# Where a kernel's end loads its MLP results and runs its last value products

## The chip, the cores and the metric

The kernel runs on one core of one Trainium2 chip. The time is the device time of that core in microseconds (us): the median of three runs, 750.84 us (750.7 to 752.2). The profile is one execution of the same program.

## The reference

One row block of 2048 tokens with 512 features goes through two branches that a gate mixes.

```python
def _A_ref(x, wqkv, wo):                      # H = 32 heads of 16, window W = 256
    q, k, v = ...                             # x @ wqkv, split into heads
    scores = jnp.einsum("bhqd,bhkd->bhqk", q, k) * (Dh ** -0.5)
    mask = (idx[:, None] - idx[None, :] >= 0) & (idx[:, None] - idx[None, :] < W)
    p = _softmax(jnp.where(mask[None, None], scores, -1e9), axis=-1)
    o = jnp.einsum("bhqk,bhkd->bhqd", p, v)
    return (...o...) @ wo

def _B_ref(x, w1, b1, w2, b2):                # F = 1792
    h = _gelu(jnp.einsum("bsd,df->bsf", x, w1) + b1)
    return jnp.einsum("bsf,fd->bsd", h, w2) + b2

g = _sigmoid((x * gate_w).sum(-1, keepdims=True))
return g * _A_ref(...) + (1 - g) * _B_ref(...)
```

## The kernel before

**Two streams of work share TensorE.** The dense stream is a generator, `dense()`: the projections to q, k and v for four row blocks `t` of 512 tokens, then the MLP in eight turns (four row blocks, two halves of the hidden features; products `u` into the hidden features, `y` out of them), then `final(t)`, which multiplies the normalised attention output `ot` of a row block with `wo` (products `a`), mixes in the gated MLP result and stores. Each dense product is three matmuls (`mm3`, lines 108 to 110), because operands are kept as a high and a low part.

**The attention stream** runs over units `u`: eight groups `g` of four heads, and in each 16 blocks `kb` of 128 keys. For each unit there are four matmuls `sm` (line 519) whose row maxima VectorE takes, and, 12 units later (`LEAD`), four matmuls `st` (line 564) whose exponentials ScalarE writes to `pt` (line 586) and VectorE clips to the window (line 574, in the last 12 units). Every fourth unit a block of about 47 value products `pv` (line 608) multiplies the `pt` of six key blocks with the values in `vbuf`. The result `nd` is stored to DRAM; `att_norm` later loads the denominators (`den`), takes their reciprocal on VectorE (line 650), stores that (`RD`), loads numerators and reciprocals (`num`, `rb`), multiplies, and stores `OT`, from which `load_part` fetches `ot`.

**What sets the order.** Python writes all engines' instructions in one pass, and each engine runs its own in that order. A loop over `u` writes `st` and value products and lets the dense stream fill in `step / 4` ns of products after each; smaller work (exponentials, stores, `att_norm`) is put on a heap with `after(ns, ...)` and written when a running count of nominal ns passes its due time. So a change of position in the loop moves instructions on every engine. All loads and stores are issued by SyncE, on one DMA queue.

**PSUM.** The pools `st` and `sm` have three buffers each. The value products take one buffer from each of them, so with `st` before them they use the buffer of the `st` three places back. The dense products alternate between two buffers `d`.

**The end.** The maxima run 12 units ahead, so they are through before the last 12 units of the other loop. `load_y(t)` then fetches the MLP results of row blocks 0, 1 and 2 from DRAM (`YB`) into the buffers that the maxima used (`qd`, `kd`): six loads of 512 KB. In the version before, that is written at units 9, 11 and 13 of the last group, two loads at each. Value products of unit `u - 1` are written inside unit `u`, right behind its third `st`, and those of the last unit stand behind the loop, ahead of all of `final`.

```python
if op == "p" and i == PVAT and u >= 1:     # line 944
    att_pvs(u - 1)
if u - NU + NKB in (9, 11, 13):            # line 958
    load_y((u % NKB - 9) // 2)
att_pvs(NU - 1)                            # line 960, behind the loop
```

Of the kernel before, what the change touches and what calls it, by code (L numbers as in the profile page):

```python
# [32 lines left out]
def gated_mix(ctx: ExitStack, tc: tile.TileContext, x, wqkv, wo, w1, b1, w2, b2, gate_w, out):  # L33
# [12 lines left out]
    def f32(ap):  # L46
        return ap.bitcast(F32)
# [67 lines left out]
    def after(ns, fn, *args):  # L115
        now[1] += 1
        heapq.heappush(todo, (now[0] + ns, now[1], fn, args))

    def step_todo():
        due, _, fn, args = heapq.heappop(todo)  # L120
        keep, now[0] = now[0], due
        fn(*args)
        now[0] = max(keep, due)

    def tick(ns):
        now[0] += ns
        while todo and todo[0][0] <= now[0]:
            step_todo()

    def need(*keys):  # L130
        for key in keys:
            while key not in done:
                step_todo()
# [319 lines left out]
    def ready(t, g_, k):  # L453
        need(*[("qk", t, k * NC + 2 * (g_ // 4) + a) for a in range(2)])

    def part(st, g_, s):

        return heads(st, g_)[s].rearrange("d u a c -> (d u) (a c)")
# [23 lines left out]
    def load_kd(g_, c):  # L482
        for t in range(max(c - 1, 0), c + 1):
            ready(t, g_, 1)
            k0 = 0 if t == c else T - W
            at = W if t == c else 0
            src = heads(SK[t], g_)[:, :, :, :, k0:].rearrange("s d u a c -> (s d u) a c")
            nc.sync.dma_start(f32(kd[0:96, slot(g_, c), :, at:at + T - k0]), src)

    def load_qd(g_, c):  # L490
        ready(c, g_, 0)
        put_pairs([f32(qd[48 * s:48 * s + 48, slot(g_, c)]) for s in range(2)], SQ[c], g_)

    def load_qs(g_, c):
        ready(c, g_, 0)
        need(("v", NT - 2, NB - 1))
        for s in range(2):
            v = f32(qs[64 * s + 4:64 * s + 52, :, c * T:(c + 1) * T])
            nc.sync.dma_start(v, part(SQ[c], g_, s).rearrange("r (a c) -> r a c", a=2))
# [8 lines left out]
    def att_max(g_, b, i):  # L508

        if b % RB == 0 and (g_, b // RB) not in Ms:  # L510
            Ms[g_, b // RB] = sb.tile([128, 2 * RB, 2], F32, tag="M", bufs=2, name=f"M{g_}_{b}")
        M = Ms[g_, b // RB]
        hb, pr = divmod(i, 2)
        c, n = b // NB, slot(g_, b // NB)
        j = 2 * (b % NB) + hb
        w = min(64 * (2 * b + hb + 1), W + 64)
        k1 = 64 * (j + 1) + W
        p = ps.tile([128, 320], F32, tag="sm", bufs=3, name=f"sm{g_}_{b}_{i}")
        nc.tensor.matmul(p[:, :w], qd[0:96, n, pr, 128 * j:128 * (j + 1)], kd[0:96, n, pr, k1 - w:k1],  # L519
                         start=True, stop=True)  # L520
        junk = cs.tile([128, 320], BF16, tag="jm", bufs=1, name=f"jm{g_}_{b}_{i}")

        def red():
            nc.vector.tensor_tensor_reduce(junk[:, :w], p[:, :w], mask[:, 320 - w:320], 1.0, -3e38,  # L524
                                           ALU.add, ALU.max, M[:, 2 * (b % RB) + hb, pr:pr + 1])
            done.add(("max", g_, b, i))
        tick(w / 2.4 + 13)
        after(100, red)
# [63 lines left out]
    def att_pvs(u):  # L592

        g_, kb = divmod(u, NKB)
        c, k = divmod(kb, NB)
        if k < NB - 1:
            return
        blocks = list(range(max(kb - 5, 0), kb + 1))
        pairs = list(zip(blocks, reversed(blocks) if c else blocks))
        n = g_ * NT + c - 1  # L600
        if n >= 0:
            need(("nd", *divmod(n, NT)))
        pv = [ps.tile([128, T], F32, tag=tag, bufs=3, name=f"pv{g_}_{c}_{tag}") for tag in ("st", "sm")]

        def mm(b, i, hf, q, e, rhs, start, stop):
            r = 64 * (1 ^ hf ^ i % 2)
            v = 68 * (b % NB) + 17 * (i % 2 * 2 + i // 2)
            nc.tensor.matmul(pv[r // 64][32 * i:32 * i + 32, q - c * T:e - c * T],  # L608
                             vts[g_, b // NB][r:r + 64, v:v + 32], rhs(r),
                             start=start, stop=stop, skip_group_check=True, tile_position=(r, 32 * i))  # L610
        if c == 0:
            for i in range(4):
                mm(0, i, 1, 0, 64, lambda r: nil[r:r + 64].broadcast_to([64, 64]), True, False)
        for j, pair in enumerate(pairs):
            for hf, b in enumerate(pair):
                need(("pt", g_, b, hf))
            ends = []
            for i in range(4):
                for hf, b in enumerate(pair):
                    k0 = b * 128 + hf * 64  # L620
                    q, e = max(k0, c * T), min(k0 + W + 64, S, (c + 1) * T)
                    mm(b, i, hf, q, e, lambda r: pts[g_, b][r:r + 64, hf, i // 2, q - k0:e - k0],
                       j == 0 and not (c == 0 and hf == 1), j == len(pairs) - 1)
                    ends.append(e - q)
            tick(max(ends) * 1.6 + 40)
        nd = sb.tile([128, T], F32, tag="tmp", bufs=3, name=f"nd{g_}_{c}")

        def half():
            nc.scalar.activation(nd, pv[0], AF.Copy)

        def ev():
            nc.vector.tensor_add(nd, nd, pv[1])
            after(HOLD if g_ * NT + c < NQ - 4 else 800, store)

        def store():
            nc.sync.dma_start(ND[c][g_ // 2][g_ % 2], nd)
            done.add(("nd", g_, c))
            if g_ % 2 == 1:
                after(NORM if g_ * NT + c < NQ - 4 else 3500, att_norm, c, g_ // 2)
        after(100, half), after(700, ev)  # L640
# [200 lines left out]
    def load_y(t):  # L841

        need(*[("y", 1, t, b) for b in range(NB)])
        for i in range(NB // 2):
            if t < 2:
                v = f32(qd[:, t, i]).rearrange("p (j f) -> p j f", j=2)
            else:
                v = f32(kd[:, i, :, 0:T])
            nc.sync.dma_start(v, YB[t].rearrange("(i j p) f -> i p j f", j=2, p=128)[i])
            for j in range(2):  # L850
                ybs[t * NB + 2 * i + j] = v[:, j]
# [44 lines left out]
    def dense():  # L896
        for t in range(NT):
            yield from qkv(t)
        for n in range(len(TURNS)):
            yield from mlp(n)  # L900
        yield None
        for t in range(NT):
            yield from final(t)

    stage = ["qk"]
    run = dense()
# [13 lines left out]
    NU = NG * NKB  # L920
# [5 lines left out]
    for u in range(-LEAD, NU):  # L926
        m = u + LEAD
        gm, bm = divmod(m, NKB)
        step = STEP if u >= 0 else STEP0
        for i in range(4):  # L930
            if i == 1 and m % NB == 0 and NB <= m < NU - NB:
                load_kd(*divmod(m // NB + 1, NT)), load_qd(*divmod(m // NB + 1, NT))
            if i % 2 == 0:
                pair = (i, i + 1) if stage[0] != "u" else (i,)
            elif len(pair) == 2:
                continue
            else:
                pair = (i,)
            for op, i in [(op, k) for k in pair for op in ORDER[:3]] + [("f", k) for k in pair]:
                if op == "s" and u >= 0:  # L940
                    att_exp(u // NKB, u % NKB, i)
                if op == "m" and m < NU:
                    att_max(gm, bm, i ^ XOR)
                if op == "p" and i == PVAT and u >= 1:
                    att_pvs(u - 1)
                if op == "f":
                    fill(step / 4)
        if m < NU and bm % RB == RB - 1:
            after(900, att_rows, gm, bm // RB)
        if m % NB == QAT % NB and QAT <= m < QAT + NKB:  # L950
            load_qs(0, (m - QAT) // NB)
        if u % NB == 0 and NB <= u < NU - NB:
            load_ks(*divmod(u // NB + 1, NT))
        if u % NB == 2 and NB < u < NU - 3 * NB:
            load_qs(*divmod(u // NB + 3, NT))
        if u % NB == 0 and u >= 0:
            att_load_v(*divmod(u // NB, NT))
        if u - NU + NKB in (9, 11, 13):
            load_y((u % NKB - 9) // 2)
    att_pvs(NU - 1)  # L960
    for c in run:
        tick(c or 0)
    tick(1e9)


# [6 lines left out]
NKB = S // 128  # L972
# [3 lines left out]
LEAD = 12  # L976
# [19 lines left out]
AHEAD = 9e3  # L996
STEP0 = 2750.0
PVAT = 2
STEP = 2330.0
_TC = dict()  # L1000
_INS = ["A_x", "A_wqkv", "A_wo", "B_w1", "B_b1", "B_w2", "B_b2", "gate_w"]
# [18 lines left out]
```

## Time and profile before

| | |
|---|---|
| median of three runs | 750.84 us (750.7 to 752.2) |
| profiled execution: its time, its span | 750.61 us, 748.9 us |
| TensorE busy | 734.0 us, 98% of the span |
| VectorE, ScalarE, GpSimd busy | 520.6, 421.7, 372.4 us |
| granted TensorE clock | 1.00 over the whole span |
| chain that ended last | TensorE 84%, DMA 4%, VectorE 4%, ScalarE 3%, issue 3% |

The span is the profiled stretch of that execution; 1.7 us of its time lie outside. A matmul is listed with the time from its start to its modelled end, but the next one starts before that end: a product of 128x512 is listed at about 0.39 us and the following one starts 0.23 us later. Distances between starts are therefore what counts on TensorE. A time in brackets at a row is the engine's idle time ahead of it and what ended that.

### The profile page before, as it was taken

How to read it: one execution, taken by the hardware profiler on the slowest of the kernel's cores; microseconds unless marked ns; L12 is line 12 of the kernel's file. 1: busy time of each engine (PE TensorE's matmuls, PEld its weight loads, DVE VectorE, ACT ScalarE, POOL GpSimd, SP SyncE). 2: the span in 40 equal slices, each digit the busy share in tenths (PEclk: the TensorE clock that was granted, in tenths of full speed). 3: DMA queues.
4: the chain of work that ended last, by engine and by line, in shares of the span. 5: the costliest groups of instructions: out<-in, count | busy, mean ns of one | idle time of the engine just before them, and what ended most of it. 6: DMA issues, size and time to landing. Idle time of an engine off the chain costs nothing.

```text
span 748.9 us, 17963 instructions
## 1 busy us (share of the span) xinstructions
PE 734.0 (98%) x6129; PEld 606.7 (81%) x6129; DVE 520.6 (70%) x1567; ACT 421.7 (56%) x972; POOL 372.4 (50%) x846
## 2 busy tenths in 40 slices
PE   9999999998999999999999999999999999999998
PEld 7888888876788888888887887888888888878787
DVE  4532325799768867986798689768867886784552
ACT  4434532358537845764695478447735853784541
POOL 4200000339756865876587567747765875630000
PEclk9999999999999999999999999999999999999999
DMA  9889798997995777799676989996799799438682
GB/s 316 329 268 407 257 392 277 273 312 182 273 251 133 172 229 211 176 227 249 164 174 152 241 215 230 259 235 155 171 268 244 180 238 239 136 88 262 217 287 106
DMA packets 179259, 172.12 MB, mean 230 GB/s; under 512 B 56672, under 2 KB 122976, under 8 KB 179168
## 3 DMA queue, kind: packets, MB, share of 16 engines
q1 hardware_dynamic: 179168, 170.97, 81.3%
q8 instruction: 49, 0.80, 0.5%
q14 instruction: 42, 0.34, 0.2%
HBM read 108.53 MB, written 62.39 MB: 228 GB/s over the span
## 4 chain that ended last, share of the span: by engine, by line
PE 84%; DMA 4%; DVE 4%; ACT 3%; issue 3%; SPq 1%; POOL 1%; DVEq 0%; ACTq 0%; POOLq 0%
PE sm L519 9%; PE st L564 8%; PE pv_sm L608 7%; PE y L108 6%; PE y L109 6%; PE y L110 6%; PE u L108 6%; PE u L109 5%; PE u L110 5%; PE qk L110 4%; PE qk L108 4%; PE qk L109 4%; PE pv_st L608 2%; PE a L108 2%; PE v L108 2%
## 5 line engine op out<-in xcount | busy, mean ns | idle before, releaser
L524 DVE CUSTOM_DVE_ANT_0 jm<-sm,mask 128x320 bf16<-128x320 f32 (+4 forms) x512 | 238.0, 465 | 95.6 <-PE sm L519 61.2
L580 POOL TENSOR_SCALAR_AFFINE_SELECT pt<-pt 64x256 f32<-64x256 f32 (+1 forms) x538 | 228.1, 444 | 108.6 <-ACT pt L586 98.1
L586 ACT ACTIVATE pt<-st 128x320 f32<-128x320 f32 (+4 forms) x512 | 199.6, 424 | 138.7 <-PE st L564 136.1
L519 PE MATMUL sm<-kd,qd 96*128 96x320 f32 (+4 forms) x512 | 154.1, 312 | 6.0 <-DVE M L524 5.1
L564 PE MATMUL st<-qs,ks 128*128 128x320 f32 (+4 forms) x512 | 154.4, 309 | 1.7 <-ACT pt L586 1.7
L546 POOL CAST qs<-tt 4x256 fp32r<-4x256 f32 x256 | 124.2, 485 | 52.7 <-DVE tt L539 42.0
L519 PEld LDWEIGHTS sm<-kd,qd 96*128 96x128 f32 x512 | 96.5, 188 | 32.8 <-DVE M L524 13.5
L564 PEld LDWEIGHTS st<-qs,ks 128*128 128x128 f32 x512 | 97.5, 190 | 18.5 <-ACT pt L586 2.9
L108 PE MATMUL y<-w,h 128*128 128x512 f32 x224 | 88.6, 395 | 0.0
L109 PE MATMUL y<-w,h 128*128 128x512 f32 x224 | 88.1, 393 | 0.0
L110 PE MATMUL y<-w,h 128*128 128x512 f32 x224 | 87.9, 393 | 0.0
L108 PE MATMUL u<-mx,w 128*128 128x512 f32 x196 | 80.0, 408 | 0.0
L109 PE MATMUL u<-mx,w 128*128 128x512 f32 x196 | 77.4, 395 | 0.0
L110 PE MATMUL u<-mx,w 128*128 128x512 f32 x196 | 77.1, 393 | 0.0
L608 PE MATMUL pv_st<-pt,vbuf 64*32 64x320 f32 (+4 forms) x1408 | 73.3, 346 | 1.5 <-ACT pt L586 1.0
L608 PE MATMUL pv_sm<-pt,vbuf 64*32 64x320 f32 (+4 forms) x1408 | 74.2, 347 | 0.2
L608 PEld LDWEIGHTS pv_sm<-pt,vbuf 64*32 64x32 f32 x1408 | 51.2, 106 | 19.3 <-issue 2.2
L325 DVE TENSOR_TENSOR qke<-qk,qke 128x512 fp32r<-128x512 f32 x32 | 22.0, 689 | 46.9 <-ACT qke L322 31.1
L322 ACT ACTIVATE qke<-qk 128x512 fp32r<-128x512 f32 x32 | 19.1, 598 | 56.2 <-PE qk L110 30.3
L110 PEld LDWEIGHTS y<-w,h 128*128 128x128 f32 x224 | 42.1, 188 | 9.8
L608 PEld LDWEIGHTS pv_st<-pt,vbuf 64*32 64x32 f32 x1408 | 46.2, 106 | 1.8 <-ACT pt L586 1.1
L338 POOL MEMSET vx<- 128x32 f32 x16 | 2.4, 155 | 88.9 <-DMA SK<-qke 30.7
(148 smaller groups left out, 1334.7 us busy)
## 6 DMA issues: line engine op xcount, KB each, us to landing
kd<-SK SPq DMA_DIRECT2D x32, 384.0 KB
qs<-SQ SPq DMA_DIRECT2D x64, 192.0 KB
mx<-XT SPq DMA_DIRECT2D x24, 512.0 KB
SQ<-qke SPq DMA_DIRECT2D x16, 512.0 KB
SK<-qke SPq DMA_DIRECT2D x16, 512.0 KB
ND<-nd SPq DMA_DIRECT2D x32, 256.0 KB
raw_w<-in_B_w_dram SPq DMA_DIRECT2D x28, 256.0 KB
ks<-SK SPq DMA_DIRECT2D x32, 192.0 KB
```

The costliest lines, as they stand in the source:

```text
L108: nc.tensor.matmul(p, lh, rh, start=first, stop=False)
L109: nc.tensor.matmul(p, lh, rl, start=False, stop=False)
L110: nc.tensor.matmul(p, ll, rh, start=False, stop=last)
L322: nc.scalar.activation(e[:, h], p, AF.Copy)
L325: nc.vector.tensor_sub(e[:, 1 - h], p, f32(e[:, h]))
L519: nc.tensor.matmul(p[:, :w], qd[0:96, n, pr, 128 * j:128 * (j + 1)], kd[0:96, n, pr, k1 - w:k1], start=True, stop=True)
L524: nc.vector.tensor_tensor_reduce(junk[:, :w], p[:, :w], mask[:, 320 - w:320], 1.0, -3e38, ALU.add, ALU.max, M[:, 2 * (b % RB) + hb, pr:pr ...
L546: nc.gpsimd.tensor_copy(dst, src.unsqueeze(1).broadcast_to([4, 2, RB, 32]))
L564: nc.tensor.matmul(p[:, :w], ks[:, slot(g_, kb // NB), pr, at:at + 128], qs[:, pr, k0:k0 + w], start=True, stop=True)
L580: nc.gpsimd.affine_select(out=v, in_=v, pattern=[[0, v.shape[1]], [1 - 2 * e, 64]], compare_op=ALU.is_ge, fill=0.0, base=-e, channel_multi ...
L586: nc.scalar.activation(pt[:, hf, pr, :w], p[:, :w], AF.Exp, scale=SCALE)
L608: nc.tensor.matmul(pv[r // 64][32 * i:32 * i + 32, q - c * T:e - c * T], vts[g_, b // NB][r:r + 64, v:v + 32], rhs(r), start=start, stop=s ...
```

## The change

Three things move; no computation is added or removed.

- The six loads of `YB` are written at units 4, 5 and 6 of the last group, two at each, instead of 9, 11 and 13.
- For `u > NU - LEAD` (the last 11 units of the loop) the value products of unit `u - 1` are written at the end of unit `u`, behind its fourth `st` and the dense products that follow it, but ahead of the load of the next values.
- The last value products stand inside the first product of `final(0)`: behind `HELD + 1 = 3` of its four parts of three matmuls.

```diff
-                if op == "p" and i == PVAT and u >= 1:
+                if op == "p" and i == PVAT and 1 <= u <= NU - LEAD:
                     att_pvs(u - 1)
...
+        if u > NU - LEAD:
+            att_pvs(u - 1)
         if u % NB == 0 and NB <= u < NU - NB:
             load_ks(*divmod(u // NB + 1, NT))
...
         if u % NB == 0 and u >= 0:
             att_load_v(*divmod(u // NB, NT))
-        if u - NU + NKB in (9, 11, 13):
-            load_y((u % NKB - 9) // 2)
-    att_pvs(NU - 1)
-    for c in run:
+        if u - NU + NKB in (4, 5, 6):
+            load_y(u - NU + NKB - 4)
+    for n, c in enumerate(run):
         tick(c or 0)
+        if n == HELD:
+            att_pvs(NU - 1)
     tick(1e9)
...
+HELD = 2
```

On SyncE's queue, behind the keys and values that unit 4 loads (`ks`, `vbuf`), the version before had the normalisation of row block 0 (its last quarter of the heads):

```order
L505 DMA vbuf<-SV_88 128x8x34
L646 DMA den_3_10046<-ND_3_102 128x1x32
L653 DMA RD_3_118<-den_3_10046 128x32
L658 DMA num_3_10177<-ND_3_102 128x1x512
L658 DMA rb_3_10179<-RD_3_118 128x1x512
L636 DMA ND_3_106<-nd_1_10190 128x512
```

Now it has, at the same place:

```order
L505 DMA vbuf<-SV_88 128x8x34
L849 DMA qd<-YB_135 128x2x512 x2
L849 DMA qd<-YB_136 128x2x512 x2
L646 DMA den_3_10050<-ND_3_102 128x1x32
L849 DMA kd<-YB_137 128x2x512 x2
L653 DMA RD_3_118<-den_3_10050 128x32
L658 DMA num_3_10161<-ND_3_102 128x1x512
L658 DMA rb_3_10163<-RD_3_118 128x1x512
```

Four loads of 512 KB have come ahead of the load of `den`, and two more ahead of the store of its reciprocal.

On TensorE, the first of the moved value products (`pv_1`) stood between the third and the fourth `st` of unit 8 in the version before:

```order
L110 MATMUL y_10_10099<-w_9_6354,h_9_9842 128x512
L564 MATMUL st_8_2_10129<-qs,ks 128x320
L608 MATMUL pv_1_sm<-pt_2_9787,vbuf 32x64
L608 MATMUL pv_1_st<-pt_7_10077,vbuf 32x64
L608 MATMUL pv_1_st<-pt_2_9787,vbuf 32x64
```

Now `st_8_3` and six dense matmuls come first:

```order
L110 MATMUL y_10_10105<-w_9_6354,h_9_9842 128x512
L564 MATMUL st_8_2_10135<-qs,ks 128x320
L564 MATMUL st_8_3_10137<-qs,ks 128x320
L108 MATMUL y_10_10105<-w_10_6421,h_10_9908 128x512
L109 MATMUL y_10_10105<-w_10_6421,h_10_9908 128x512
L110 MATMUL y_10_10105<-w_10_6421,h_10_9908 128x512
L108 MATMUL y_10_10105<-w_11_6511,h_11_10012 128x512
L109 MATMUL y_10_10105<-w_11_6511,h_11_10012 128x512
L110 MATMUL y_10_10105<-w_11_6511,h_11_10012 128x512
L608 MATMUL pv_1_sm<-pt_2_9787,vbuf 32x64
L608 MATMUL pv_1_st<-pt_7_10083,vbuf 32x64
```

The block has moved back by one `st` and six dense matmuls; `pv_2` moves in the same way by one `st` and three.

The last value products (`pv_3`) followed the last `y` directly; now nine matmuls of the first product `a` of `final(0)` stand between:

```order
L110 MATMUL y_13_10418<-w_13_6718,h_13_10104 128x512
L108 MATMUL a_0_0_10489<-wo_9824,ot_10295 128x512
L109 MATMUL a_0_0_10489<-wo_9824,ot_10295 128x512
L110 MATMUL a_0_0_10489<-wo_9824,ot_10295 128x512
L108 MATMUL a_0_0_10489<-wo_9895,ot_10295 128x512
L109 MATMUL a_0_0_10489<-wo_9895,ot_10295 128x512
L110 MATMUL a_0_0_10489<-wo_9895,ot_10295 128x512
L108 MATMUL a_0_0_10489<-wo_10006,ot_10295 128x512
L109 MATMUL a_0_0_10489<-wo_10006,ot_10295 128x512
L110 MATMUL a_0_0_10489<-wo_10006,ot_10295 128x512
L608 MATMUL pv_3_sm<-pt_10_10241,vbuf 32x64
L608 MATMUL pv_3_st<-pt_15_10453,vbuf 32x64
```

The last three matmuls of that `a` come behind the value products.

## The prediction

> **What bounds the kernel now.** I read the page first, then TensorE's waits, then the end of the trace engine by engine in order of time. The page says that TensorE is nearly always busy, and the list of its waits over the whole span says how little idle time there is to win at the end:
>
> ```profile
> PE 734.0 (98%) x6129; PEld 606.7 (81%) x6129; DVE 520.6 (70%) x1567; ACT 421.7 (56%) x972; POOL 372.4 (50%) x846
> ...
> PEclk9999999999999999999999999999999999999999
> ```
>
> ```profile
> PE sm L519 <- DVE M L524: 5.1, 10, 1.0
> PE st L564 <- ACT pt L586: 1.7, 3, 1.0
> PE pv_st L608 <- ACT pt L586: 1.6, 2, 1.0
> PE pv_st L608 <- DVE pt L574: 0.5, 1, 0.5
> ```
>
> The columns are total, count and longest, in us; no wait of TensorE is longer than 1.0. The change touches nothing ahead of 662 us, so only waits behind that can go. They are these, on TensorE's timeline (start, listed duration, idle time ahead in brackets):
>
> ```profile
> 669.64 0.30 PE L564 MATMUL st<-qs,ks 128*128 128x320 f32 x1
> ...
> 671.15 0.25 PE L608 MATMUL pv_st<-pt,vbuf 64*32 64x64 f32 x2 [0.98 <-ACT pt L586]
> ...
> 673.47 0.41 PE L564 MATMUL st<-qs,ks 128*128 128x320 f32 x1
> ...
> 675.11 0.31 PE L564 MATMUL st<-qs,ks 128*128 128x320 f32 x1
> ...
> 676.10 0.45 PE L564 MATMUL st<-qs,ks 128*128 128x320 f32 x2
> ...
> 685.42 0.30 PE L564 MATMUL st<-qs,ks 128*128 128x320 f32 x1
> ...
> 687.98 0.41 PE L564 MATMUL st<-qs,ks 128*128 128x320 f32 x1
> ...
> 693.88 0.25 PE L564 MATMUL st<-qs,ks 128*128 128x192 f32 x1
> 695.11 0.36 PE L564 MATMUL st<-qs,ks 128*128 128x192 f32 x1 [0.98 <-ACT pt L586]
> ...
> 698.32 0.40 PE L110 MATMUL y<-w,h 128*128 128x512 f32 x1
> ...
> 699.43 0.25 PE L608 MATMUL pv_st<-pt,vbuf 64*32 64x64 f32 x2 [0.48 <-DVE pt L574]
> ...
> 701.75 0.50 PE L108 MATMUL a<-wo,ot 128*128 128x512 f32 x1
> ```
>
> Three holes: 671.15 (the first value products, `pv_1`), 695.11 (a late `st`) and 699.43 (the last value products, `pv_3`). `pv_2`, between the rows at 685.42 and 687.98, has none. Two `st` together are listed at 0.45 and one at 0.30, so the second starts 0.15 behind the first; 2.56 less that 0.15 leaves 2.41 for an undisturbed block with its two changes of matmul kind. The holes are 2.44 us together, 0.33% of the time, and that is about the most that the change can win.
>
> **Hole one: `pv_1` behind six dense matmuls.** ScalarE and VectorE at that place:
>
> ```profile
> 667.73 0.42 DVE L574 TENSOR_TENSOR pt<-pt,cut 128x256 f32<-128x256 f32 x1
> 668.06 0.34 DVE L650 RECIPROCAL den<-den 128x32 f32<-128x32 f32 x1
> 668.33 0.63 DVE L737 TENSOR_TENSOR h<-x1h,h 128x512 fp32r<-128x512 f32 x1
> ```
>
> ```profile
> 668.99 0.69 ACT L719 ACTIVATE x1h<-u,b1c 128x512 f32<-128x512 f32 x1 [0.71 <-DVE h L737]
> ...
> 670.66 1.09 ACT L586 ACTIVATE pt<-st 128x320 f32<-128x320 f32 x3
> ```
>
> This is one chain without slack: reciprocal of `den`, low part of `h_11`, ScalarE's `x1h` of `h_13` (it needs that `x1` buffer), two more activations, the exponential of `st_8_0`, and 0.49 us behind that one's start `pv_1` gets its PSUM buffer. `pv_1` waits for the buffer of `st_8_0`, the `st` three places back. In the new order the instruction behind `st_8_2` is `st_8_3`, and it is now the one that takes the buffer of `st_8_0`. So the same wait ends at the same exponential, only with another instruction behind it. The six dense matmuls that could cover it stand behind `st_8_3`. This hole I count at no gain, and about 0.1 of loss, since the first few products of `pv_1` ran before the wait. VectorE's and ScalarE's order up to here is the old one.
>
> **The loads of `YB`: what they push back.** SyncE, with its queue in the old order, and the DMA traffic (the last two columns of each window are the mean busy share of the 16 engines and GB/s):
>
> ```profile
> 661.63 0.53 SPq L505 DMA_DIRECT2D vbuf<-SV  x1
> 662.26 0.63 SPq L646 DMA_DIRECT2D den<-ND  x1
> ```
>
> ```profile
> 660.00:664.50 4.50, 4.50 (x22) 3.49 (x21) 4.25 (x8) 4.50 (x12) 2.27 (x4) 1.00 0.73 180
> 664.50:668.50 4.00, 4.00 (x19) 2.90 (x19) 2.92 (x7) 3.77 (x10) 0.00 (x0) 1.00 0.01 2
> 680.50:683.00 2.50, 2.50 (x14) 2.16 (x13) 1.45 (x3) 1.38 (x5) 0.00 (x0) 1.00 1.00 370
> 680.00:692.00 12.00, 12.00 (x143) 9.62 (x142) 5.21 (x12) 5.74 (x15) 0.00 (x0) 1.00 1.00 325
> ```
>
> Before, `den` (16 KB) is issued at 662.26 behind `ks` and `vbuf`; the traffic ends at 664.5 and VectorE takes `den` at 668.06 without waiting, some 3 us later. Now four loads of 512 KB are issued from 662.26 on, ahead of it. They wait for nothing but old transfers; at 0.5 each (the pair at 695.51 below took 0.98) they are all issued by 664.3, and their data follows that of `vbuf` at 664.5. 4 x 524 KB = 2.10 MB at 370 GB/s is 5.67 us, to 670.2. That the small load then comes out behind them, and not past them, I read from two places where `YB` loads were ahead of something:
>
> ```profile
> 685.51 8.62 DMA ot<-OT
> ```
>
> ```profile
> 695.51 0.98 SPq L849 DMA_DIRECT2D kd<-YB  x2
> 698.58 0.61 SPq L646 DMA_DIRECT2D den<-ND  x1
> ```
>
> ```profile
> 701.70 0.35 DVE L650 RECIPROCAL den<-den 128x32 f32<-128x32 f32 x1 [1.73 <-DMA den<-ND]
> ```
>
> The first, from the chain of waits, is a load of 256 KB issued two microseconds behind a pair of `YB` loads: 8.62 us from issue to landing. In the second a `den` behind a pair reaches VectorE 3.1 us after its issue. So I put the landing at 670.4 (an estimate: end of the traffic plus 0.2). The reciprocal then starts 2.35 us late, and as VectorE runs in order, `h_11`, ScalarE's chain and the exponential of `st_8_0` move by the same 2.35. `st_8_3` starts at 671.15 + 2.35 = 673.50 instead of the wait's old end. TensorE is idle from 669.94 to there, 3.6 us. Behind it come 0.25 for `st_8_3`, six dense matmuls (673.72 to 675.11 in the old order: 1.39) and `pv_1` at 2.41, so `st_9_0` starts at 677.55 where it was 675.11: **+2.45**. Bounds: at 325 GB/s, the mean of a long mixed stretch, the data ends at 670.95 and the term is +3.2; if `den` were not held at all it would be +0.1.
>
> The two further loads (`kd`, 1.05 MB, 2.8 us) stand ahead of the store of the reciprocal, so that `rb` is issued not at 669.87 but near 673.5:
>
> ```profile
> 669.87 0.58 SPq L658 DMA_DIRECT2D rb<-RD  x1
> ...
> 693.50 0.59 SPq L658 DMA_DIRECT2D rb<-RD  x1
> ```
>
> ```profile
> 680.92 0.68 DVE L662 TENSOR_TENSOR num<-num,rb 128x512 f32<-128x512 f32 x1
> ```
>
> VectorE used it 11 us after its issue, and will come 2.45 later too; about 10 us are left, so I cost this at nothing. If that cover were gone, VectorE's clips behind it would be late by the rest. Further down the queue each load of `vbuf` waits for the value products that read the old values. The one for `pv_2` now waits until `pv_1` ends at 677.5, but behind it stands the store of `pv_1`'s own result. The one for `pv_3` now stands ahead of the second `num` and `rb` and waits for the end of `pv_2`, 688.0 + 2.45 + 0.84 (an `st` and three dense matmuls) = 691.3. That `rb` was issued at 693.50 before, so nothing is late by it.
>
> **Hole two, 695.11.** It is the other end of the same loads:
>
> ```profile
> 694.15 0.63 ACT L706 ACTIVATE ot<-ot 128x512 fp32r<-128x512 f32 x1 [2.45 <-DMA ot<-OT]
> ```
>
> ScalarE stood at the load of `ot` that took 8.62 us, with the exponentials of `pt_14` behind it, and `st_14_3` waited for one of them. Without `YB` traffic between 677 and 692 that load is issued about 686 and lands within some 3 us, near 689. ScalarE came to it at 694.15 - 2.45 = 691.7 and now comes later still. The wait goes: from 693.88 to 695.11 are 1.23 where a pair of `st` is issued 0.15 apart, so **-1.08**. Nothing is next in line there: `st_14_3`'s buffer is freed by an exponential that can now run at once. The lower bound is no gain, if another wait stood behind.
>
> **Hole three, 699.43.** From the last `y` (698.32 + 0.23 = 698.55) to the first `a` (701.75) are 3.20, against 2.41 for an undisturbed block: 0.79 of loss, from a clip of `pt_15` on VectorE that is late because `ot`'s split is. Now nine matmuls, 2.05 us, come first, and the late `ot` is early. **-0.75**. Their cover costs something else: `pv_3` ends 2 us later within the stream, so its `nd` and the last row block's normalisation start later, here by 2.5 us in all. At the other end of that chain stand
>
> ```profile
> 730.60 0.63 ACT L706 ACTIVATE ot<-ot 128x512 fp32r<-128x512 f32 x1 [3.07 <-DMA ot<-OT]
> ```
>
> ```profile
> 735.46 0.68 DVE L709 TENSOR_TENSOR ot<-ot 128x512 fp32r<-128x512 f32 x1
> ```
>
> `ot` is ready on ScalarE at 731.2, and VectorE's split follows at 735.46 behind another instruction: 4.2 us of slack for a delay of 2.5. I count nothing.
>
> **Sum.** +2.45 - 1.08 - 0.75 = +0.6 us. The profiled execution took 750.61 (span 748.9), 0.2 under the median of 750.84; on the median that is 751.4.
>
> **Rivals.**
>
> - *`den` is not held up* (its small packets pass the big loads, or the loads start at once in the engines that are free before 664.5 and run faster than 370 GB/s). For it: the DMA queue is idle from 664.5 to 668.5, and 3 us of delay were free. Against it: the two rows above. It decides when `den` lands by 668.1. Then only +0.1 - 1.08 - 0.75 = -1.7: 749.1 us.
> - *The long hole costs more than its length: the clock.* This is the other side. The new hole of 3.6 us is over three times the longest wait in the trace, and all of this trace runs at a granted clock of 1.00, so no row shows what such a gap does. If it made the granted clock fall to half for what comes behind it, the `st`, the six dense matmuls (1.6 us) and, at the most, `pv_1` (2.4 us) would take twice as long: +1.6 to +4.0 on top of +0.6, so 753.0 to 755.4. It decides at the length of the gap, which the DMA rate sets. [...]
> - *`den` later still*, at 325 GB/s or because SyncE waits for a transfer's slot among the four issues: +3.2 instead of +2.45, with the clock untouched: 752.2; with a normalisation of the last row block that slips past its 4.2 us of slack as well, up to 753.
> - *The value products' move is only a relabelling* is part of the forecast for hole one; for hole three it would take away 0.75 and give 752.1.
>
> **How the numbers follow.** A measurement of this kernel tells about 0.2%, 1.5 us, from no change. My forecast, 750.8 to 752.0, has a chance of 0.5. `den` in time: 0.13, faster. The clock: 0.13, slower. `den` later still or another late wait: 0.19, half of it beyond 752.3. Hole three not won: 0.05, no change. So faster 0.13, within 0.2% 0.58, slower 0.29. The range of 749.5 to 753.0 leaves out most of the first rival and the upper part of the clock and of the later `den`, together about two in ten.
>
> **What would show it.** On the changed kernel's VectorE the reciprocal at about 668 should carry a wait of some 2.4 us for the DMA of `den`. TensorE should show one hole of about 3.5 us ahead of an `st`, its largest, ended by ScalarE's exponential. ScalarE's 2.45 at `ot` and TensorE's two later holes should be gone, and `final` should run without a wait. I am wrong if that reciprocal doesn't wait, if the granted clock drops behind the hole, or if a wait appears at the last row block's `ot`.

## The result, and the profile after

| | before | changed |
|---|---|---|
| median, us | 751.45 (749.93 to 753.0, 6 runs) | 756.05 (755.23 to 758.68, 6 runs) |
| profiled execution: time, span, us | 750.61, 748.9 | 756.78, 755.1 |
| ratio, 95% interval | | 1.0069 [1.0056, 1.0083] |

The changed kernel is slower by 0.7%, 4.6 us by the medians. I had forecast 751.4, within 749.5 to 753.0.

TensorE's waits over the whole span of the changed kernel (total, count, longest in us):

```profile
PE st L564 <- ACT pt L586: 5.7, 3, 4.9
...
PE a L108 <- DVE ao L883: 0.5, 1, 0.5
```

Before, no wait behind the program's first microseconds was longer than 1.0 (one of 1.2 stands at its very start, which the prediction's list leaves out). Now one of 4.9 stands there, and a small one of a kind that was not in the list: a product `a` of `final` that waits for its PSUM buffer (`L883` reads the buffer out). Here is the long one on TensorE's timeline:

```profile
671.28 0.30 PE L564 MATMUL st<-qs,ks 128*128 128x320 f32 x1
676.53 0.41 PE L564 MATMUL st<-qs,ks 128*128 128x320 f32 x1 [4.94 <-ACT pt L586]
676.78 0.58 PE L108 MATMUL y<-w,h 128*128 128x512 f32 x1
677.16 0.63 PE L109 MATMUL y<-w,h 128*128 128x512 f32 x1
...
682.11 0.56 PE L564 MATMUL st<-qs,ks 128*128 128x320 f32 x2
```

The row at 671.28 is `st_8_2`, which began at 669.64 before; the 1.64 between them come from the stretch ahead of 662 us, where the program is the same. (Two waits of that stretch, near 206 and 445 us, are longer in some executions than in others, whatever the kernel: near 206 none before, 0.71 here and 1.21 in e11_pv2_only, near 445 none before, 0.83 here and 1.67 in e8_last_back.) So I measure everything behind it from the start of `st_8_2`, and call the distance from there to the end of the span the tail: 748.9 - 669.64 = 79.26 before, 755.1 - 671.28 = 83.82 now, **+4.56**, close to the 4.6 of the medians. That agreement is in part luck. A stretch of 3.41 us at half clock (the second window below) takes 0.0023 off the mean granted clock of a run of 755 us. The profiled execution has 0.998, so one such stretch; the other five executions of the changed kernel have 0.995, about two, and where the second lies in them is not on record.

Two things are to be seen in the rows. The hole ahead of `st_8_3` is 5.25 from start to start. And behind it dense matmuls start 0.43 apart that elsewhere start 0.23 apart: they run at half rate. The windows say the same (PEclk, DMA share and GB/s are the last three columns). The first begins at 666.14, which is the 664.5 of the prediction, 1.64 later in this trace:

```profile
666.14:672.00 5.86, 5.45 (x25) 3.83 (x23) 2.57 (x5) 3.81 (x10) 0.00 (x0) 1.00 1.02 359
...
676.83:680.24 3.41, 3.41 (x39) 2.23 (x45) 2.66 (x5) 2.33 (x5) 0.00 (x0) 0.50 0.71 210
```

Followed back, the hole ends at ScalarE's exponential, that one's chain at VectorE's `h_11`, and that at the reciprocal, which stood 3.62 at the load of `den`:

```profile
674.37 0.69 ACT L719 ACTIVATE x1h<-u,b1c 128x512 f32<-128x512 f32 x1 [4.42 <-DVE h L737]
...
676.04 1.09 ACT L586 ACTIVATE pt<-st 128x320 f32<-128x320 f32 x3
```

```profile
673.43 0.35 DVE L650 RECIPROCAL den<-den 128x32 f32<-128x32 f32 x1 [3.62 <-DMA den<-ND]
```

Where the 4.56 come from, step by step along TensorE, each place by its distance from `st_8_2` in the two traces:

- `st_9_0`, behind `pv_1`: 682.11 - 671.28 = 10.83, before 675.11 - 669.64 = 5.47. **+5.36**: the hole and the half rate.
- The 15th matmul `a` of `final`, behind `pv_3`: 38.89 (its row below), before 35.41. +3.48, so holes two and three between them gave back **1.88**.
- The end: +4.56, so **1.08** was lost again inside `final`, nearly all of it around 734 us:

```profile
706.26 0.39 PE L110 MATMUL a<-wo,ot 128*128 128x512 f32 x1
708.91 0.50 PE L108 MATMUL a<-wo,ot 128*128 128x512 f32 x1
...
710.17 0.39 PE L110 MATMUL a<-wo,ot 128*128 128x512 f32 x1
```

```profile
734.21 0.39 PE L110 MATMUL a<-wo,ot 128*128 128x512 f32 x1
735.11 0.50 PE L108 MATMUL a<-wo,ot 128*128 128x512 f32 x1 [0.51 <-DVE ao L883]
```

The first pair shows `pv_3` inside `final` without a hole: 2.65 from `a` to `a`, which is the undisturbed block of 2.41 and a matmul. (A block of the last group is 96 matmuls in both traces, not about 47.)

### The profile page after: what moved, and what is told of

Read it like the earlier page. It is cut to its first block, busy times and chain, and to the rows that moved or that the text cites. A ratio compares the mean times of both kernels' runs of the same rounds, so it can differ in the third digit from the quotient of the medians.

```text
span 755.1 us, 17960 instructions
## 1 busy us (share of the span) xinstructions
PE 734.5 (97%) x6129; PEld 604.7 (80%) x6129; DVE 519.5 (69%) x1567; ACT 422.6 (56%) x972; POOL 372.5 (49%) x846
## 4 chain that ended last, share of the span: by engine, by line
PE 79%; DMA 7%; DVE 4%; issue 3%; ACT 3%; SPq 2%; POOL 1%; DVEq 0%; ACTq 0%; POOLq 0%
PE sm L519 9%; PE st L564 8%; PE pv_sm L608 7%; PE y L108 6%; PE y L110 6%; PE y L109 6%; PE u L108 5%; PE u L109 5%; PE u L110 5%; PE qk L110 4%; PE qk L108 4%; PE qk L109 4%; PE v L108 2%; PE v L110 2%; PE v L109 2%
```

## The experiments

All medians are against the kernel before on the same chip in the same rounds (750.85, 751.1 and 751.07 in the three sets). "Tail" is one profiled execution against 79.26. The "late gap" is the longest distance between two starts of `a` in `final`, where 0.23 is normal (none: below 0.6); the 2.64 in which `pv_3` itself stands there is left out. "Last products" says where `pv_3` stands.

| | loads at | `pv_1`, `pv_2` | last products | median | ratio [95%] | tail | hole ahead of `st_8_3` or in `pv_1` | late gap |
|---|---|---|---|---|---|---|---|---|
| before | 9, 11, 13 | old | ahead of `final` | 751.45 | 1 | 0 | 1.20 | none |
| changed | 4, 5, 6 | moved | in `final` | 756.05 | 1.0069 | +4.6 | 5.25 | 0.90 |
| e1_products | 9, 11, 13 | moved | in `final` | 753.14 | 1.0029 [1.0019, 1.0039] | +2.4 | 1.54 | 2.71 |
| e2_loads | 4, 5, 6 | old | ahead | 755.37 | 1.0057 [1.0044, 1.007] | +3.3 | 4.01 | none |
| e3_loads678 | 6, 7, 8 | moved | in `final` | 751.47 | 1.001 [0.9995, 1.0024] | +2.1 | 1.51 | 2.37 |
| e4_filled | 4, 5, 6 | moved | in `final` | 753.48 | 1.0038 [1.0025, 1.0051] | +2.0 | 2.21 | none |
| e5_loads678_only | 6, 7, 8 | old | ahead | 750.21 | 0.9987 [0.9975, 1.0] | -1.1 | 1.19 | none |
| e6_rcp_later | 4, 5, 6 | moved | in `final` | 751.0 | 0.9999 [0.9981, 1.0016] | +3.3 | 1.31 | 3.65 |
| e7_last_only | 9, 11, 13 | old | in `final` | 752.78 | 1.0016 [1.0004, 1.0027] | +1.2 | 1.19 | 1.59, 0.98 |
| e8_last_back | 6, 7, 8 | moved | ahead | 749.82 | 0.9986 [0.9974, 0.9998] | -1.5 | 1.51 | none |
| e9_rcp3_later | 6, 7, 8 | moved | in `final` | 751.42 | 1.0006 [0.9993, 1.002] | -0.3 | 1.51 | 1.53 |
| e10_loads567 | 5, 6, 7 | moved | in `final` | 750.1 | 0.9988 [0.9973, 1.0003] | -1.1 | 2.31 | none |
| e11_pv2_only | 6, 7, 8 | `pv_2` moved | ahead | 751.34 | 0.9997 [0.9985, 1.001] | -1.1 | 1.23 | none |
| e12_nd_first | 6, 7, 8 | moved | in `final` | 752.14 | 1.0003 [0.999, 1.0016] | -0.8 | 1.51 | 1.08 |

Median and tail don't agree everywhere, because the unchanged stretch ahead of `st_8_2` adds between 0 and 4 us to a single execution (`st_8_2` starts between 669.46, in e5_loads678_only, and 673.71, in e4_filled), and because one execution need not be the usual one. The profile of e3_loads678 has a mean granted clock of 0.995, but eight of its twelve executions have 1.0 (749.38 to 751.85 us); that of e1_products has 0.998, but eight of twelve have 0.999 or 1.0 (751.58 to 753.63 us). So most executions of these two have no half-rate stretch, and the sizes of the late gap below, read from the profiles, need not be the usual ones. For the mechanism the rows of the tail decide, for the verdict the medians.

### The halves of the change alone

Of the changed kernel, only the products moved (loads back at 9, 11, 13):

```diff
-        if u - NU + NKB in (4, 5, 6):
-            load_y(u - NU + NKB - 4)
+        if u - NU + NKB in (9, 11, 13):
+            load_y((u % NKB - 9) // 2)
```

> The changed kernel with the six loads of YB put back to units 9, 11 and 13; the value products stay at their new places. Theory (the loads ahead of den do the harm): the reciprocal on VectorE near 668 runs without a wait, the hole ahead of st_8_3 is about 1.1 us as in the kernel before, the granted clock stays at 1.00, the hole at the last value products is gone, and the time is 0.3 to 1.0 us under the kernel before (ratio 0.9985 to 0.9996). Rival (the products' new places do the harm: st_8_3 takes the buffer that the value products took): a hole of 4 to 5 us ahead of st_8_3 and 4 to 5 us more than the kernel before (ratio 1.006).

Of the kernel before, only the loads moved:

```diff
-        if u - NU + NKB in (9, 11, 13):
-            load_y((u % NKB - 9) // 2)
+        if u - NU + NKB in (4, 5, 6):
+            load_y(u - NU + NKB - 4)
```

> The kernel before with the six loads of YB at units 4, 5 and 6; no value products are moved. Theory: VectorE's reciprocal waits 3 to 4 us for den, the value products pv_1 wait 4 to 5 us for the exponential of st_8_0, the clock falls behind that hole, the load of ot is not late any more: 3.5 to 5.5 us over the kernel before (ratio 1.005 to 1.007). Rival (products): within 0.15% of the kernel before or up to 1 us faster.

The loads alone give 1.0057, as expected, with a hole of 4.01 inside `pv_1`. The products alone I had expected to gain 0.3 to 1.0; they cost 2.3 (1.0029). So there was a second mechanism that the prediction doesn't have. The longest of TensorE's waits behind 640 us in that kernel:

```profile
PE a L108 <- DVE ao L883: 2.3, 1, 2.3
```

It is the same kind of wait as the small one of the changed kernel, only larger. It is taken up below.

### The long hole

Den ahead of the loads (loads at 6, 7, 8):

```diff
-        if u - NU + NKB in (4, 5, 6):
-            load_y(u - NU + NKB - 4)
+        if u - NU + NKB in (6, 7, 8):
+            load_y(u - NU + NKB - 6)
```

> The changed kernel with the loads at units 6, 7 and 8, so that the load of den is issued ahead of all of them; all else as changed. Theory: no wait of the reciprocal near 668, hole ahead of st_8_3 about 1.1 us, clock 1.00, ScalarE's wait for ot near 694 gone or shorter than 1 us: 0.5 to 1.8 us faster than the kernel before (ratio 0.9976 to 0.9993). If a late normalisation alone is to blame for the small wait in the last products, that wait is gone too. Rival (products): as slow as the changed kernel, ratio 1.006.

The hole is 1.51 and the reciprocal near 670 doesn't wait, as expected; but the late gap came again, and the gain with it went. One pair of loads ahead of `den` instead of two:

```diff
-        if u - NU + NKB in (4, 5, 6):
-            load_y(u - NU + NKB - 4)
+        if u - NU + NKB in (5, 6, 7):
+            load_y(u - NU + NKB - 5)
```

> The changed kernel with the YB loads at units 5, 6, 7: on SyncE one pair of loads stands ahead of row block 0's den instead of two, two pairs behind it. If den is held only by what is ahead of it on the queue: the pair is through about 4.5 us behind 664 (half of the changed kernel's 9), the reciprocal waits for 0.5 us or less and the hole stays near 1.5 to 2.0, so the time is that of the loads at 6, 7, 8 (ratio 1.000 to 1.002). If the pairs issued behind it share the engines with it, den lands 2 us later still, the hole is 3 us or more and half rate follows: ratio 1.003 to 1.006.

SyncE's queue in the changed kernel and in this one:

```profile
663.86 2.37 SPq L849 DMA_DIRECT2D qd<-YB  x4
666.27 0.64 SPq L646 DMA_DIRECT2D den<-ND  x1
```

```profile
662.36 1.17 SPq L849 DMA_DIRECT2D qd<-YB  x2
663.62 0.63 SPq L646 DMA_DIRECT2D den<-ND  x1
664.30 1.14 SPq L849 DMA_DIRECT2D qd<-YB  x2
665.48 1.02 SPq L849 DMA_DIRECT2D kd<-YB  x2
```

```profile
669.00 0.35 DVE L650 RECIPROCAL den<-den 128x32 f32<-128x32 f32 x1 [0.70 <-DMA den<-ND]
```

With 1 MB ahead of it `den` takes 5.4 us from issue to VectorE, with 2 MB 7.2 us (669.00 - 663.62 and 673.43 - 666.27), and the four loads behind it in the second kernel don't push it back by the two further microseconds that I had put on sharing. So it is held by what is ahead of it. The wait of 0.70 and the hole of 2.31 are a little above what I had set (0.5 and 2.0); the ratio is lower than expected, which fits that this profile has no late gap.

Row block 0's reciprocal later on VectorE, with the loads as in the change:

```diff
-        for ns, fn in zip(DIVS[c == NC - 1], (rcp, keep, back, mul, store)):
+        for ns, fn in zip(LATER if (t, c) == (0, NC - 1) else DIVS[c == NC - 1], (rcp, keep, back, mul, store)):
...
+LATER = (9000, 10200, 13000, 17500, 19000)
```

> The changed kernel, YB loads where the change puts them, but row block 0's reciprocal written later, so that on VectorE it stands behind the low parts of h_11 and h_12 (about 675) instead of ahead of them. Theory (the late den costs only because VectorE runs in order): den lands as late as in the changed kernel (673.4) and nothing waits for it; the hole ahead of st_8_3 is 1.5 us from start to start, as with the loads late, and no half rate follows it; the late waits in final stay, 2 to 2.7 us with half rate: ratio 1.001 to 1.0035. Rival (the DMA traffic itself holds ScalarE's or TensorE's chain there): hole of 3 us or more, ratio 1.005 or more.

```profile
669.67 0.30 PE L564 MATMUL st<-qs,ks 128*128 128x320 f32 x1
670.98 0.41 PE L564 MATMUL st<-qs,ks 128*128 128x320 f32 x1 [1.00 <-ACT pt L586]
...
675.03 0.56 PE L564 MATMUL st<-qs,ks 128*128 128x320 f32 x2
```

```profile
673.41 0.35 DVE L650 RECIPROCAL den<-den 128x32 f32<-128x32 f32 x1
```

The same loads, the same traffic, and the hole falls from 5.25 to 1.31: `st_9_0` starts at 675.03 in that trace, 5.36 behind `st_8_2`, where before it was 5.47. That settles the first part: the late `den` costs only because VectorE runs in order and `h_11` stands behind the reciprocal. The median came out at no difference, below what I expected, with times from 748.57 to 754.29; its profile has a late gap of 3.65, and I take the spread to be that gap, present in some executions and not in others. The granted clock of each run points the same way: it is 0.997 or 0.998 in three of the twelve (752.29 to 754.29 us) and 0.999 or 1.0 in the other nine (748.57 to 752.15 us). Where the half rate lay in those three is known for the profiled one alone, so this is argued, not shown.

The hole filled: fourteen matmuls whose result nobody reads, added between `st_8_2` and `st_8_3` of the changed kernel:

```diff
+                if op == "p" and i == 2 and u == NU - 8:
+                    keep_busy(FILL)
...
+    def keep_busy(n):
+        need(("w", ("wo", 0)))
+        p = ps.tile([128, T], F32, tag="sm", bufs=3, name="busy")
+        for _ in range(n):
+            nc.tensor.matmul(p, wt["wo", 0][:, 0, 0:128], wt["wo", 0][:, 0], start=True, stop=True)
...
+FILL = 14
```

> The changed kernel with 14 more matmuls of 128x512, whose result nothing reads, between st_8_2 and st_8_3, in a PSUM buffer that is free there: 3.2 us of work inside the hole of 4.9 us. Theory (the hole costs its length, and half a clock behind it): the reciprocal's wait stays at about 3.6 us and the hole ends at the same exponential, but is only 1.7 us long; the granted clock stays at 1.00, the six dense matmuls behind it are 0.23 us apart and not 0.43, and the time is 1.3 to 1.7 us under that of the changed kernel, so 2.8 to 3.6 us over the kernel before (ratio 1.0037 to 1.0048). Rival (the slow stretch has another cause than the idle time): spacing 0.43 again and ratio 1.006.

```profile
673.71 0.31 PE L564 MATMUL st<-qs,ks 128*128 128x320 f32 x1
673.86 3.36 PE L909 MATMUL busy<-wo 128*128 128x512 f32 x14
679.04 0.42 PE L564 MATMUL st<-qs,ks 128*128 128x320 f32 x1 [1.82 <-ACT pt L586]
679.30 0.39 PE L108 MATMUL y<-w,h 128*128 128x512 f32 x1
```

`st_8_3` comes 5.33 behind `st_8_2`, as late as in the changed kernel, yet the dense matmuls behind it start 0.23 apart from the first on. Against the kernel before in the same rounds this version is 2.6 us slower (753.48 against 750.85) where the changed kernel was 4.6 slower: 14 useless matmuls win 2.0. In the profiles the tail is 2.5 shorter: `st_9_0` comes 9.39 behind `st_8_2` and not 10.83, 1.4 less for the half rate, and the other 1.1 is the late gap, which was not in this profile either. The granted clock of whole runs agrees on the half rate: 1.0 in six of the eight executions here, 0.998 or less in all six of the changed kernel. (The 0.995 of the profiled execution comes from two half-rate stretches near 180 and 450 us, in the part that did not change.)

### The late gap in `final`

The first profile to show it large was that of the products alone; here is e3_loads678, with SyncE, VectorE and TensorE around it:

```profile
706.92 0.32 SPq L703 DMA_DIRECT2D ot<-OT  x1
...
708.67 0.40 SPq L636 DMA_DIRECT2D ND<-nd  x1
...
714.83 0.59 SPq L646 DMA_DIRECT2D den<-ND  x1
```

```profile
704.78 0.69 DVE L632 TENSOR_TENSOR nd<-nd,pv_sm 128x512 f32<-128x512 f32 x1 [2.65 <-ACT nd L629]
...
717.74 0.35 DVE L650 RECIPROCAL den<-den 128x32 f32<-128x32 f32 x1 [3.82 <-DMA den<-ND]
...
718.55 1.28 DVE L709 TENSOR_TENSOR ot<-ot 128x512 fp32r<-128x512 f32 x2
719.75 0.75 DVE L883 SCALAR_TENSOR_TENSOR ao<-a,g,ao 128x512 f32<-128x512 f32 x1
```

```profile
718.18 0.39 PE L110 MATMUL a<-wo,ot 128*128 128x512 f32 x1
720.55 0.50 PE L108 MATMUL a<-wo,ot 128*128 128x512 f32 x1 [1.99 <-DVE ao L883]
720.89 0.59 PE L109 MATMUL a<-wo,ot 128*128 128x512 f32 x1
721.27 0.63 PE L110 MATMUL a<-wo,ot 128*128 128x512 f32 x1
```

The last row block's `nd` is ready at 705.5, but its store is issued at 708.67, behind an `ot` load of another row block that waits for an `OT` store (SyncE's wait for it is 3.6 us in e1_products, 3.8 in the changed kernel), and behind `num` and `rb` (the rows left out between). Its `den` reaches VectorE at 717.7. There the reciprocal, a product (left out) and two splits of `ot` stand ahead of the `L883` that frees the product's PSUM buffer. TensorE stands 2.0, and then runs at half rate again.

Four runs on this. The kernel before with the last products alone moved into `final(0)`:

```diff
-    att_pvs(NU - 1)
-    for c in run:
+    for n, c in enumerate(run):
         tick(c or 0)
+        if n == HELD:
+            att_pvs(NU - 1)
...
+HELD = 2
```

> The kernel before with one of the three moves only: the last value products inside final(0). Theory (the late products cost a new wait: their nd is written to DRAM behind a load of ot that waits for an OT store, so the last row block's den lands near 717, and its reciprocal stands on VectorE ahead of the L883 that frees TensorE's product buffer): hole three is won (-0.75), a wait of TensorE's a for L883 of 2.0 to 2.7 us appears near 718, and the matmuls behind it run at half rate for about 3 us (+1.4): ratio 1.002 to 1.0045. Rival (the late wait of the earlier runs came from the moved pv_1 and pv_2 or from the loads): no such wait, -0.75 alone, ratio 0.9985 to 0.9995.

And the last products alone put back, with the loads at 6, 7, 8:

```diff
+    att_pvs(NU - 1)
-    for n, c in enumerate(run):
+    for c in run:
         tick(c or 0)
-        if n == HELD:
-            att_pvs(NU - 1)
```

> The changed kernel with the YB loads at units 6, 7, 8 and the last value products back in their place ahead of final(0); pv_1 and pv_2 stay moved. Theory as above: no wait of a for L883 near 718, no long wait ahead of st_8_3, hole two gone, hole three back at up to 0.8: ratio 0.9975 to 0.9992. Rival (late wait from elsewhere): the wait of 2 us near 718 stays, ratio 1.001 to 1.003.

One move alone brings the gap (1.59 and a second of 0.98, without half rate; I had expected 2.0 to 2.7 with it; 1.0016, just below the range), and taking that move alone back removes it. Over all traces: none of the five kernels with the last products ahead of `final` has a gap there, seven of the nine with them inside it have one. Behind 640 us e8_last_back has one wait of TensorE left:

```profile
PE st L564 <- ACT pt L586: 1.2, 1, 1.2
```

The last row block's reciprocal later on VectorE, loads at 6, 7, 8:

```diff
-        for ns, fn in zip(DIVS[c == NC - 1], (rcp, keep, back, mul, store)):
+        for ns, fn in zip(LAST if (t, c) == (NT - 1, NC - 1) else DIVS[c == NC - 1], (rcp, keep, back, mul, store)):
...
+LAST = (7000, 7600, 9000, 17000, 18500)
```

> The changed kernel with the YB loads at units 6, 7, 8, and the reciprocal of the last row block's den written later, so that on VectorE it stands behind the next product's L883 and L709. Nothing else is moved on purpose. Theory (VectorE's order behind the late den is what holds TensorE): the den lands as late as before, near 717.7, but the wait of a for L883 is under 0.3 us and no half rate follows: holes two and three are won, ratio 0.996 to 0.9985. Rival (the a product is held by something else, for example by ot's late load): the wait near 718 stays, ratio 1.000 to 1.002.

```profile
717.76 0.34 DVE L650 RECIPROCAL den<-den 128x32 f32<-128x32 f32 x1
...
727.38 0.69 DVE L709 TENSOR_TENSOR ot<-ot 128x512 fp32r<-128x512 f32 x1 [2.38 <-ACT ot L706]
```

```profile
728.60 0.39 PE L110 MATMUL a<-wo,ot 128*128 128x512 f32 x1
730.13 0.50 PE L108 MATMUL a<-wo,ot 128*128 128x512 f32 x1 [1.15 <-DVE ao L883]
```

The reciprocal no longer waits and the gap at 718 is gone, as the theory has it. But a gap of 1.53 has come at 728.6, where the split of `ot` (`L709`) that itself came late stands ahead of an `L883`: everything of the last row blocks' normalisation is late, and the next instruction of it stands in the way. The time stayed where it was (1.0006), which is the rival's number for another reason.

The `nd` store earlier on SyncE, VectorE's order unchanged:

```diff
-            after(HOLD if g_ * NT + c < NQ - 4 else 800, store)
+            after(HOLD if g_ * NT + c < NQ - 4 else 400 if g_ * NT + c == NQ - 1 else 800, store)
...
-            after(REACH, done.add, ("o", t, c))
+            after(LATE if (t, c) == (1, NC - 1) else REACH, done.add, ("o", t, c))
...
+LATE = 3500
```

> The changed kernel with the YB loads at units 6, 7, 8, and on SyncE the store of the last row block's nd ahead of the loads of num, rb and ot that stood ahead of it; VectorE's order is the same. Theory (the late den comes from SyncE's queue: the nd store stands behind an ot load that waits 3.6 us for an OT store): nd is stored near 705.6 instead of 708.7, den's reciprocal comes near 715 instead of 717.7, the wait of a for L883 is 1 us or less, no half rate, no later wait: ratio 0.996 to 0.999. Rival (the den is late for another reason, e.g. the traffic): the reciprocal stays near 717 and the hole at 2 us or more: ratio 1.000 to 1.002.

```profile
706.17 0.32 SPq L636 DMA_DIRECT2D ND<-nd  x1
...
707.93 1.81 SPq L703 DMA_DIRECT2D ot<-OT  x4
710.27 0.59 SPq L646 DMA_DIRECT2D den<-ND  x1
```

```profile
717.12 0.35 DVE L650 RECIPROCAL den<-den 128x32 f32<-128x32 f32 x1 [2.14 <-DMA den<-ND]
```

Counted from `st_8_2` (671.64 in e3_loads678, 672.30 here) the store is 3.2 us earlier and `den` is issued 5.2 earlier, but it now takes 6.9 us from issue to VectorE, with four `ot` loads of 256 KB right ahead of it, where it took 2.9 in e3_loads678. The reciprocal is 1.3 earlier, the gap shrinks to 1.08 and the half rate is gone; yet the ratio of 1.0003 is the rival's. By these two profiles SyncE's order was part of the cause, not all of it; the medians do not separate them.

### What is left of the gain

The kernel before with the loads at 6, 7, 8 and no product moved, and the same with `pv_2` alone moved behind its unit's fourth `st`:

```diff
-        if u - NU + NKB in (9, 11, 13):
-            load_y((u % NKB - 9) // 2)
+        if u - NU + NKB in (6, 7, 8):
+            load_y(u - NU + NKB - 6)
```

> The kernel before with the YB loads at units 6, 7, 8 and no product moved: den of row block 0 is issued ahead of all of them. Theory (the long hole of the changed kernel comes from loads ahead of den; loads behind it are free and take away hole two): reciprocal at 668 without a wait, hole one 1.0 as before, hole two gone, hole three 0.5 to 0.8: ratio 0.998 to 0.9993. Rival (early YB loads cost something themselves, by traffic or by SyncE): ratio 1.000 or more.

```diff
-                if op == "p" and i == PVAT and u >= 1:
+                if op == "p" and i == PVAT and u >= 1 and u != NU - NB:
...
+        if u == NU - NB:
+            att_pvs(u - 1)
```

> The kernel before with the YB loads at units 6, 7, 8 and only the middle block of value products (pv_2) moved behind its unit's fourth st; pv_1 and pv_3 stand where they stood. Theory: hole one as before (1.2 from start to start), hole two gone by the loads, hole three gone because everything behind pv_2 on VectorE and ScalarE shifts; no late wait: -1.9 us, ratio 0.9965 to 0.9985. Rival (hole three needs the other moves too): hole three of 0.8 stays, ratio 0.998 to 0.9995.

Loads behind `den` take away hole two, as expected; hole three stays at 0.79 in both, so the theory of the second was wrong: `pv_2` alone does nothing for it. It goes when `pv_1` and `pv_2` are moved (e8_last_back) or `pv_3` is (e7_last_only). The version that beats both kernels is e8_last_back: 749.82, ratio 0.9986 [0.9974, 0.9998], with `st_9_0` 0.1 later and holes two and three gone (-1.5 in the tail). At 0.14% its interval just excludes no change, the only one of twelve that does so on this side; it is less than the 0.2% that the prediction took as the bound, and the runs do not separate it from e5_loads678_only (0.9987) or e10_loads567 (0.9988).

## Why the prediction was wrong

- **`den` behind the loads.** The mechanism came out as written: SyncE's order, VectorE's order, ScalarE's chain, `st_8_3`. The size did not. I put the start of `st_8_3` 2.35 behind the old end of the wait, at 673.50; in that trace's time it came at 676.53 - 1.64 = 674.89, 1.39 later. The rate was not what failed: from 666.14 (the 664.5 of the prediction) to 672.00 the engines moved 359 GB/s against my 370, and in the packet records of the trace the 1024th packet of 2 KB, which makes 2.10 MB, starts at 671.81, which is 670.17 in the old time against my 670.2. The step that failed is "end of the traffic plus 0.2". The 128 packets of `den` start between 671.33 and 672.95, and VectorE's reciprocal 0.48 behind the last of them, at 673.43: 1.6 behind the 2.10 MB, not 0.2. Why the last of them come so late is not shown by any run. The bound that I had kept, +3.2 at 325 GB/s, is near the +3.8 of the hole alone, but for another reason.
- **The clock.** This was the rival with the chance of 0.13, and it came true, together with that of a later `den`. From the start of `st_8_3` to `st_9_0` I had 0.25 + 1.39 + 2.41 = 4.05; it took 682.11 - 676.53 = 5.58. The 1.5 lie just under the rival's 1.6 to 4.0, since full rate came back after 3.41 us (676.83 to 680.24), inside `pv_1`. e4_filled shows that the term hangs on the idle time: with the hole filled it is gone. In the sum I had set this term to zero, with a hole of 3.6 us in hand and no row of so long a gap: nothing ahead of the result showed the half clock on which the rival rests, or how likely it was, and the window from 676.83 to 680.24 now shows 0.50. Together these two make +5.36 where I had +2.45.
- **Hole one** was rightly no gain; with the loads out of the way the same gap is 0.3 longer than before (1.51 against 1.20 in e3_loads678), and `st_9_0` comes 0.1 later (5.57 against 5.47 behind `st_8_2`), as I had put it.
- **Holes two and three** were right: 1.88 against 1.83. The split was right too: the loads alone win hole two (e5_loads678_only).
- **`rb` and `num` at no cost** held: no wait for them shows in TensorE's list, and VectorE's product of the two (`L662`) runs at 688.1 without a wait.
- **"`pv_3` ends 2 us later ... I count nothing"** failed. I had looked at the one place where the chain ends, the last `ot` on ScalarE, and found 4.2 us of slack. I had not looked at the instructions of the same chain on the way, which stand in VectorE's order ahead of `L883`: the reciprocal and the splits. In the changed kernel they cost 1.1; without the long hole the products alone cost 2.3 in all (e1_products). That the long hole hid the rest by delaying TensorE as well fits the table, where the profiles with a hole of 2.2 or more and `pv_3` in `final` have a late gap of 0.90 or none, but was not tested by itself. "`final` should run without a wait" was the sign that I had named, and it did not hold.
- **The sum**: +5.36 - 1.88 + 1.08 = +4.56, against my +0.6.

## What to carry to other kernels

Before a big load is written earlier, list the small loads that follow it on the same queue and, for each, what stands behind its first reader on that reader's engine; the time it loses is worked out from the bytes ahead of it and a measured rate (here 2.10 MB and 359 GB/s), plus the time from there to its reader, which was 1.6 us here and not 0.2. When work is delayed "with slack", follow every instruction of its chain on each in-order engine, since each of them can stand ahead of something that TensorE waits for (1.99 us at `L883` in e3_loads678), and the slack at the end says nothing of that. And a wait of TensorE can cost more than its length (1.5 us more here, 1.6 in e1_products, 1.7 in e3_loads678 and e6_rcp_later, each the time lost by the half rate behind the gap). Its length alone does not say whether it will: a gap of 1.82 in e4_filled did, one of 2.31 in e10_loads567 did not.

## What the runs showed of the hardware

The gap that brings the half rate. From `st_8_2` on, gaps between two starts of 1.5, 1.53, 1.59, 2.21 and 2.31 us on TensorE kept full rate, and gaps of 2.37, 2.71, 3.65, 4.01 and 5.25 us brought half rate. That looks like a line between 2.31 and 2.37, but the stretch ahead of it in the same traces takes the line away. In e4_filled, which kept its rate behind 2.21, a gap of 1.82 lost it:

```profile
445.33 0.40 PE L110 MATMUL u<-mx,w 128*128 128x512 f32 x1
447.14 0.41 PE L519 MATMUL sm<-kd,qd 96*128 96x320 f32 x1 [1.42 <-DVE M L524]
```

```profile
445.60:449.02 3.42, 1.92 (x9) 1.40 (x9) 3.28 (x11) 2.91 (x7) 1.83 (x4) 1.00 0.84 209
449.02:452.43 3.41, 3.41 (x12) 2.82 (x11) 3.12 (x11) 2.18 (x6) 0.81 (x3) 0.50 0.56 169
```

So did a gap of 2.03 in e3_loads678 (at 161.91), and in e4_filled even two of 1.04 and 0.76 close together (at 175.64 and 178.20), while 2.07 in e8_last_back (at 443.44) did not. What is the same everywhere is the half-rate stretch itself. These are the two of e3_loads678:

```profile
164.56:167.97 3.41, 3.41 (x11) 2.89 (x10) 3.27 (x12) 1.91 (x4) 1.15 (x2) 0.50 1.04 264
720.93:724.34 3.41, 3.41 (x10) 2.67 (x9) 0.82 (x2) 0.00 (x0) 0.00 (x0) 0.50 0.68 171
```

By the granted clock all eight of these stretches in the traces last 3.41 us, whatever the gap; in the changed kernel it is 0.50 from 676.830 to 680.243, for 3.413 us. The two in e3_loads678 begin 556.37 us apart and the two in e4_filled (179.36 and 449.02) 269.66: 163.0 and 79.0 times 3.413. So in these two traces the drops keep to a grid of 3.41 us, and the drop is not always at once: behind the gap of 1.82 it came 1.88 us after the work went on (449.02 against 447.14). How much idle time brings a drop stays open. In the 3.41 us ahead of a drop TensorE was idle for 1.1 to 3.4 us, and in only one of the eight, e2_loads, for the whole of it; yet in the changed kernel 1.8 us of idle time in one such step (670.00 to 673.42, where the clock stayed at 1.00) brought none.
